# Gated linear attention and a mixture of experts: when the next group's x is split, and when the sums of H and L are added up

## The chip, the cores and the metric

The kernel runs on one core of one Trainium2 chip. The metric is the device time of one execution in microseconds, as the median of three runs. PE is TensorE, DVE is VectorE, ACT is ScalarE; PEld is PE's loading of weights.

## The reference

Two blocks follow one another. The first is a recurrence over 768 positions for each of 4 batches and 8 heads of 48 channels; the second is a sum of four two-layer networks (experts) on 3072 rows of 384, each weighted by a normalised probability:

```python
for t in range(S):
    state = alpha[:, :, t, :, None] * state + np.einsum('bhd,bhe->bhde', k[:, :, t], v[:, :, t])
    y[:, :, t] = np.einsum('bhd,bhde->bhe', q[:, :, t], state)
...
x = np.ascontiguousarray(attn_out.transpose(0, 2, 1, 3)).reshape(B * S, H * D)
...
p = domain_probs / (domain_probs.sum(-1, keepdims=True) + 1e-09)
for e in range(E):
    h = np.maximum(x @ w1[e], 0.0)
    out += p[:, e:e + 1] * (h @ w2[e])
```

Here w1[e] is 384 x 1024 and w2[e] is 1024 x 384. Everything is float32.

## The kernel before

**Tiling.** The 3072 rows are 24 blocks (units) of 128 rows. They are taken in seven groups of 2, 4, 4, 4, 4, 4 and 2 blocks, numbered 0 to 6. For each group the main loop (L704) runs over the four experts. For each expert it computes the first layer (`up`, eight tiles of 128 hidden channels, each for all rows of the group) and then the second (`down`, over the rows in turns of one or two blocks). The recurrence of the blocks of the next group (`attention`, a generator with 17 steps) is worked off meanwhile.

**Three parts of a number.** A product of 128x128 by 128x384 takes PE 0.33 us with float32 operands (ten start in 3.3 us at 157.0) and 0.18 us with operands of the type float32r[...]. So the kernel writes a number as three float32r parts: H (in the code `top`), the number times 1 − 1/8192 and rounded by the type; L (`low`), the number minus H; and D (`dif`), H/4096 − L. The product of two numbers is then got from three products of like parts: H by H and L by L go into one sum in PSUM, D by D into another, and the result is the first sum times 1 + 1/4096 plus the second. In `up` the two sums are `one` and `two`, in `down` they are `ops0` and `ops1`; the factor 1 + 1/4096 sits in `p_fine`, which is `p_all` times it. The first layer works in this way in groups 1 to 5 and in most of group 6, the second layer in groups 2 to 5. Elsewhere they use whole float32 numbers.

**The split of x.** `split_x` (L451) makes the three parts of the next group's x, one of three chunks of 128 channels at a time: `split` has ACT write H (L242), then DVE write L (L243) and D (L244). It is called during the last expert's `down` of a group, through a list `between` of fractions of the way through the turns at which the calls are made (L713 to L718). With three chunks these are 1/4, 2/4 and 3/4 of the whole `down`. The tile xT that it fills has one buffer, so it can't be filled before the last `up` of the group has read the old one.

**The second layer.** In groups 2 to 5 a turn of `down` takes two blocks (slots), so there are two turns, numbered 0 and 1. A turn has 48 products of 128x128 by 128x384, in the order of `steps` (L557): H and L for the first six hidden tiles of both slots, then H and L for the last two, then D for all eight of slot 0 and all eight of slot 1. Numbered from 0, the last product of slot 0's sum of H and L is step 29, of slot 1's 31; those of D are 39 and 47. The weights and the hidden tiles are there in three parts; D of the hidden tiles for slots 2 and 3 (`make_dif`, L538) is made during turn 0, one at every fifth step.

**The banks.** `one`, `two`, `ops0` and `ops1` share four PSUM banks (tag "g"), taken in rotation. A turn of `down` uses all four: slot 0's H-and-L sum, slot 0's D sum, slot 1's two. The next turn's first product therefore goes into the bank in which slot 0's H-and-L sum of this turn stands, and waits until that has been read. It is read by `add_up` (L592), which adds each sum, scaled by the row's probability, to `acc`: with a DVE operation (L603), or, for the first expert's first sum, with an ACT copy (L601). `add_up` stands after the last D product of a slot and takes both sums of that slot, one after the other.

**What sets the order.** The order on each engine is the order of the program text as it is run (a manual schedule). `advance` (L649), called before each product of `down` and after each tile of `up`, keeps a clock of estimated costs and runs the steps of `attention` that have come due by a list that `deal` (L619) makes. Attention's last step of a group is due 6 us (`MARGIN`) before the last expert's `down`. In groups 0 and 1, `background` also runs the splitting of the weights w1 and w2 into three parts (L218 to L224), which uses ACT and DVE.

**Names in the steps of the prediction.** qb and KT (L303, L321, L322) and QT and dec (L310, L312) are attention's copies and products per level; `near` (L339) takes the scores out of PSUM; `far` (L384), `sc` (L329) and `yps` (L416) are its products on PE. Within a step of attention, ACT copies QT to qb (L303) before DVE changes QT (L310). `hidden_parts` (L526) makes H, L and half of D of a hidden tile.

Of the kernel before, what the change touches and what calls it, by code (L numbers as in the profile page):

```python
# [14 lines left out]
ACT = mybir.ActivationFunctionType  # L15
ALU = mybir.AluOpType
# [4 lines left out]
def kernel(  # L21
# [37 lines left out]
    nc = tc.nc  # L59
# [9 lines left out]
    KC = DM // P  # L69
    FCH = F // P  # L70
# [9 lines left out]
    TRIM = 1 - 1 / 8192  # L80

    j = np.arange(P)[:, None] % HALF
    n = np.arange(QUAD)[None, :]
# [15 lines left out]
    p_all = const.tile([P, NBLK, E], F32, name="p_all")  # L99
    tot = const.tile([P, NBLK], F32, name="tot")  # L100
    p_fine = const.tile([P, NBLK, E], F32, name="p_fine")
# [27 lines left out]
    xTs = {}  # L129
    xraws = {}  # L130
# [105 lines left out]
            splitting.append(making.popleft())  # L236
            next(splitting[-1])

    def split(x, out):

        top, low, dif = out
        nc.scalar.activation(out=top, in_=x, func=ACT.Copy, scale=TRIM)  # L242
        nc.vector.tensor_sub(low, x, top.bitcast(F32))  # L243
        nc.vector.scalar_tensor_tensor(out=dif, in0=top.bitcast(F32), scalar=1 / 4096.0,  # L244
                                       in1=low.bitcast(F32), op0=ALU.mult, op1=ALU.subtract)
# [202 lines left out]
        load(u + 2, "v")  # L448
        yield

    def split_x(gi, which):  # L451
        n = len(groups[gi]) * P
        if 0 in which:
            xTs[gi] = work.tile([P, 3, KC, NT], F32R, name="xT", bufs=1)
        for kc in which:
            split(xraws[gi][:, kc, :n], [xTs[gi][:, part, kc, :n] for part in range(3)])


    def up(gi, e, fc, slots=None):
# [85 lines left out]
    def down(gi, e, slots, between):  # L545


        first = (gi * E + e) * NQ
        halves_ = split2(gi, e)
        if slots[0] == 0 and makes[1](gi, e):  # L550
            making.extend(split_piece(1, first + k) for k in range(NQ))
        if slots[0] == 0 and makes[0](gi, e) and 0 < e < E - 1:
            making.extend(split_piece(0, first + k) for k in range(2, NQ))
        sums = [[ps.tile([P, DM], F32, name=f"ops{j}", tag="g", bufs=4)
                 for j in range(2 if halves_ else 1)] for _ in slots]

        kinds = [((0, 1), range(FCH - 2)), ((0, 1), range(FCH - 2, FCH)), ((2,), range(FCH))]  # L557
        steps = [(part, i, fc) for parts, tiles in (kinds if halves_ else [((3,), range(FCH))])
                 for part in parts for i in range(len(slots)) for fc in tiles]
        for n, (part, i, fc) in enumerate(steps):  # L560
            c, f = divmod(fc, FPQ)
            h = hidden[c][:, :, f, slots[i] * P:(slots[i] + 1) * P]
            advance(cost(1, gi, e) / FCH / (3 if halves_ else 1))
            while between and n >= between[0][0] * len(steps):
                between.popleft()[1]()
            if n == len(steps) // 2:
                background()
            if later and n % 5 == 4:
                make_dif(*later.popleft())
            if halves_:  # L570
                w = wt[1][first + c].rearrange("p t (c d) -> p t c d", d=DM)[:, part, f]
                nc.tensor.matmul(sums[i][part // 2], lhsT=h[:, part], rhs=w,  # L572
                                 start=(fc == 0 and part != 1), stop=(fc == FCH - 1 and part != 0))
            else:
                w = wt[1][first + c].rearrange("p (c d) -> p c d", d=DM)[:, f]
                nc.tensor.matmul(sums[i][0], lhsT=h[:, 2].bitcast(F32), rhs=w,  # L576
                                 start=(fc == 0), stop=(fc == FCH - 1))
            if part >= 2 and fc == FCH - 1:
                add_up(gi, e, slots[i], sums[i])
        background()  # L580
        if slots[-1] == len(groups[gi]) - 1:
            while makes[1](gi, e) and (making or splitting):
                background()

            for c in range(NQ):
                del wt[1][first + c]
                if c < NQ // 2:
                    load_piece(1, first + NQ + c)
                else:
                    late.append(first + NQ + c)  # L590

    def add_up(gi, e, slot, sums):  # L592
        cb, b = groups[gi][slot]
        at = b * NCB + cb
        scales = (p_fine, p_all) if split2(gi, e) else (p_all,)
        if e == 0:
            accs[cb, b] = hid.tile([P, DM], F32, name="acc", bufs=B)
        acc = accs[cb, b]
        for j, (part, scale) in enumerate(zip(sums, scales)):
            if e == 0 and j == 0:  # L600
                nc.scalar.activation(out=acc, in_=part, func=ACT.Copy, scale=scale[:, at, e:e + 1])  # L601
            else:
                nc.vector.scalar_tensor_tensor(out=acc, in0=part, scalar=scale[:, at, e:e + 1],  # L603
                                               in1=acc, op0=ALU.mult, op1=ALU.add)
        if e == E - 1:
            del accs[cb, b]
            row = b * S + cb * P
            stores.append(lambda: (nc.sync if gi == len(groups) - 1 else nc.gpsimd).dma_start(
                out=out[row:row + P, :], in_=acc))
# [45 lines left out]
    with tc.manual_schedule():  # L655
        nc.scalar.dma_start(out=ident_all, in_=nc.inline_tensor(ident_np, name="ident_c").ap())
        nc.scalar.dma_start(out=masks, in_=nc.inline_tensor(mask_np, name="masks_c").ap())
        nc.scalar.dma_start(out=p_all, in_=moe_domain_probs.rearrange("(n p) e -> p n e", p=P))
        nc.gpsimd.memset(sts[B - 1], 0.0)
        for nm in "akq":  # L660
            for r in (early[nm], apart[nm]):
                nc.gpsimd.memset(r[:, :, D:], 0.0)
        nc.gpsimd.memset(lat[HALF:, :, :HALF], 0.0)
        for t in values + blocks:
            nc.gpsimd.memset(t, 0.0)
        for t in sts[:-1]:
            nc.gpsimd.memset(t, 0.0)

        load(0, "akqv")
        load(1, "akqv")  # L670
        for i in range(NQ):
            load_piece(0, i)

        idle = ps.tile([P, P], F32, name="idle", tag="g", bufs=4)
        zeros = sts[B - 1].rearrange("p a i d -> p (a i d)")[:, :P]

        def fill(n):
            for _ in range(n):  # L680
                nc.tensor.matmul(idle, lhsT=zeros, rhs=zeros, start=True, stop=True)

        runs = [attention(u) for u in range(len(groups[0]))]
        fill(8)
        for u, n in ((0, 3), (0, 6), (0, 4), (0, 5), (0, 5), (0, 4), (0, 3), (1, 0), (0, 0), (0, 2),
                     (0, 2), (1, 2), (0, 2), (1, 0), (0, 0), (0, 4), (0, 4), (0, 0)):
            next(runs[u])
            fill(n)
        norm_probs()

        span = cost(0, 0, 0) * FCH / 2 + cost(1, 0, 0)
        waiting.extend((span * (k + 1) / 15, u, runs[u])
                       for k, u in enumerate([1, 1, 1, 0, 1, 0, *[1] * 8]))
        for fc in range(FCH):
            up(0, 0, fc, slice(0, 1))
            advance(cost(0, 0, 0) / 2)
        down(0, 0, [0], deque())
        while waiting:
            next(waiting.popleft()[2], None)
        clock = 0.0  # L700
        waiting.extend((1.0 + k, 1, runs[1]) for k in range(2))
        waiting.extend(deal())

        for gi, e in ((gi, e) for gi in range(len(groups)) for e in range(E)):  # L704
            rest = gi == e == 0
            for fc in range(FCH):
                up(gi, e, fc, slice(1, len(groups[0])) if rest else None)
                advance(cost(0, gi, e) / (2 if rest else 1))
            each = 2 if split2(gi, e) else 1
            turns = [range(k, k + each) for k in range(rest, len(groups[gi]), each)]  # L710
            for k, slots in enumerate(turns):

                between = deque()  # L713
                if e == E - 1 and gi + 1 < len(groups):
                    for kc in range(KC):
                        at = (kc + 1) / (KC + 1) * len(turns) - k
                        if 0 <= at < 1:
                            between.append((at, lambda kc=kc: split_x(gi + 1, [kc])))  # L718
                down(gi, e, slots, between)
                if gi == len(groups) - 1 and e == E - 1:  # L720
                    stores.popleft()()
        while stores:
            stores.popleft()()
# [28 lines left out]
```

## Time and profile before

| | |
|---|---|
| median of 3 runs | 1102.42 us (1102.16 to 1103.28) |
| span of the profiled run | 1098.0 us |
| PE busy | 1066.2 us, 97% of the span |
| DVE busy | 751.9 us, 68% |
| ACT busy | 561.8 us, 51% |
| mean granted clock of PE | 0.995 |
| waits of PE for `add_up` | 11.9 us, 7 times |
| waits of PE for attention (`lat`, `qb`) | 12.4 us, all before 130 us |

A row of the costliest groups gives the line, the engine, the operation, output and inputs, the shapes and the count; then the busy time and the mean duration in ns; then the idle time of the engine just before these instructions, and whose end finished most of it. In the timeline the columns are start and length in us, the engine, the line, the operation, and in brackets the idle time before it with the one that ended it. Matmul ends are modelled, so idle time of PE is better read from starts. The granted clock is 1.00 at full speed.

### The profile page before, as it was taken

What the parts mean: (1) busy time and instruction counts of PE and PEld (TensorE: products, weight loads), DVE (VectorE), ACT (ScalarE), POOL (GpSimd) and SP (SyncE); (2) the same over time, 40 slices, a digit from 0 to 9 for tenths busy, and PEclk for the clock granted to TensorE, in tenths of its full rate; (3) what the DMA queues carried; (4) which work ended last, traced back from release to release, by engine and by line L of the source; (5) the groups of instructions that cost most, each with busy time, mean ns of one, the idle gap of its engine ahead of it and who ended that gap; (6) DMA issues with size and microseconds to landing.
All of it is one profiled execution on the core that took longest, in us unless ns stands there. A gap on an engine that the chain in (4) does not pass through costs nothing.

```text
span 1098.0 us, 21700 instructions
## 1 busy us (share of the span) xinstructions
PE 1066.2 (97%) x8532; PEld 894.9 (81%) x8532; DVE 751.9 (68%) x1625; ACT 561.8 (51%) x1191; POOL 35.4 (3%) x75
## 2 busy tenths in 40 slices
PE   8889899999999999998999999899999999999998
PEld 8767677676776889897898898798988898898876
DVE  5578777656558868768778777887786876657211
ACT  5786776575556554544545435455454354223321
POOL 2000000000000000000000000000000000000000
PEclk9999999999999999999999999999999999999999
DMA  8597689877696965855758649487487468555882
GB/s 124 156 322 231 206 283 370 307 269 275 206 314 213 405 234 186 335 206 207 287 170 308 246 147 352 143 277 302 146 292 290 176 270 343 221 200 243 300 317 87
DMA packets 166197, 273.68 MB, mean 249 GB/s; under 512 B 120624, under 2 KB 140976, under 8 KB 142032
## 3 DMA queue, kind: packets, MB, share of 16 engines
q1 hardware_dynamic: 156704, 230.06, 60.4%
q0 software_dynamic: 6016, 42.08, 9.6%
q8 instruction: 67, 1.10, 0.4%
q10 hardware_dynamic: 3376, 0.17, 0.3%
q14 instruction: 34, 0.28, 0.1%
HBM read 229.81 MB, written 42.47 MB: 248 GB/s over the span
## 4 chain that ended last, share of the span: by engine, by line
PE 77%; DVE 13%; ACT 6%; issue 2%; DMA 1%; SPq 0%; ACTq 0%; DVEq 0%
PE ops L572 19%; PE one L496 18%; PE ops L576 14%; PE two L496 9%; PE sc L329 5%; PE yps L416 4%; PE one L488 3%; DVE hT L530 3%; PE tp L261 3%; DVE t L505 2%; DVE hT L538 2%; ACT qb L303 2%; ACT hT L528 2%; DVE near L339 2%; PE sps L437 1%
## 5 line engine op out<-in xcount | busy, mean ns | idle before, releaser
L572 PE MATMUL ops<-w,hT 128*128 128x384 f32 x1536 | 288.6, 342 | 12.1 <-DVE acc L603 11.9
L572 PEld LDWEIGHTS ops<-w,hT 128*128 128x128 f32 x1536 | 268.1, 190 | 17.4 <-DVE acc L603 14.5
L496 PE MATMUL one<-xT,w 128*128 128x512 f32 (+1 forms) x1104 | 275.1, 385 | 0.1
L496 PEld LDWEIGHTS one<-xT,w 128*128 128x128 f32 x1104 | 194.8, 188 | 42.1 <-issue 3.0
L503 ACT ACTIVATE t<-one 128x512 f32<-128x512 f32 (+1 forms) x184 | 102.9, 559 | 158.5 <-PE one L496 158.0
L303 ACT COPY qb<-QT 64x256 f32<-64x256 f32 x336 | 136.5, 406 | 80.2 <-DVE QT L284 46.8
L576 PE MATMUL ops<-hT 128*128 128x384 f32 x512 | 176.2, 491 | 0.0
L496 PE MATMUL two<-xT,w 128*128 128x512 f32 (+1 forms) x552 | 148.5, 377 | 0.0
L576 PEld LDWEIGHTS ops<-hT 128*128 128x128 f32 x512 | 93.9, 191 | 56.1 <-issue 0.8
L530 DVE SCALAR_TENSOR_TENSOR hT<-t,hT 128x512 fp32r<-128x512 f32 x128 | 88.7, 693 | 61.3 <-ACT hT L528 59.9
L528 ACT ACTIVATE hT<-t 128x512 fp32r<-128x512 f32 x128 | 80.9, 632 | 96.9 <-DVE t L505 95.6
L496 PEld LDWEIGHTS two<-xT,w 128*128 128x128 f32 x552 | 100.3, 188 | 19.9
L603 DVE SCALAR_TENSOR_TENSOR acc<-ops,p_all,acc 128x384 f32<-128x384 f32 x88 | 54.2, 616 | 75.2 <-PE ops L576 43.6
L538 DVE SCALAR_TENSOR_TENSOR hT<-hT 128x256 fp32r<-128x256 f32 x256 | 100.9, 422 | 4.4
L505 DVE TENSOR_TENSOR t<-t,two 128x512 f32<-128x512 f32 x128 | 87.4, 682 | 20.9 <-PE two L496 12.7
L339 DVE COPY_PREDICATED near<-masks,sc 128x256 f32<-128x256 uint8 x144 | 77.0, 535 | 21.2 <-PE sc L329 18.2
L329 PEld LDWEIGHTS sc<-qb,KT 128*64 128x64 f32 x2304 | 73.0, 139 | 9.4 <-issue 7.4
L310 DVE TENSOR_TENSOR QT<-QT,dec 128x256 f32<-128x256 f32 x144 | 60.7, 422 | 24.8 <-ACT qb L303 24.2
L508 DVE TENSOR_TENSOR hT<-t,two 128x512 f32<-128x512 f32 (+1 forms) x56 | 32.1, 573 | 66.3 <-ACT t L503 56.5
L329 PE MATMUL sc<-qb,KT 128*64 128x64 f32 x2304 | 77.2, 224 | 0.3 <-ACT qb L303 0.3
L321 ACT COPY KT<-KT 128x256 f32<-128x256 f32 x144 | 59.8, 416 | 3.0
L322 DVE TENSOR_TENSOR KT<-KT,dec 128x256 f32<-128x256 f32 x144 | 60.2, 418 | 1.7 <-PE tp L261 1.5
(79 smaller groups left out, 928.1 us busy)
## 6 DMA issues: line engine op xcount, KB each, us to landing
w<-kept SPq DMA_DIRECT2D x156, 1152.0 KB
kept<-w POOLq DMA_DIRECT2D x32, 1152.0 KB, 7.5
hT<-in_moe_w_dram SPq DMA_DIRECT2D x48, 384.0 KB
w<-in_moe_w_dram SPq DMA_DIRECT2D x60, 128.0 KB
ra<-in_alpha_dram SPq DMA_DIRECT2D x23, 192.0 KB
rk<-in_k_dram SPq DMA_DIRECT2D x23, 192.0 KB
rq<-in_q_dram SPq DMA_DIRECT2D x23, 192.0 KB
out_dram<-acc POOLq DMA_DIRECT2D x22, 192.0 KB, 5.8
```

Of the source, the lines that this page charges most:

```text
L303: nc.scalar.copy(out=qb[rows, :, i, :].rearrange("p a (b r) -> p a b r", r=m), in_=qv[rows])
L310: nc.vector.tensor_mul(qv, qv, spread(dv[:, :, :, 0], m))
L329: nc.tensor.matmul(out[HALF * s:HALF * (s + 1), 2 * p:2 * p + 2, :], lhsT=KTs[li][:, p, HALF * s:HALF * (s + 1)], rhs=qbs[li][:, p, :, QUA ...
L339: nc.vector.copy_predicated(near.rearrange("p a (b two r) -> p a b two r", two=2, r=m)[:, :, :, 1, :], mk.unsqueeze(1).broadcast_to([P, H, ...
L496: nc.tensor.matmul(out, lhsT=w[:, part, kc], rhs=xTs[gi][:, part, kc, :n], start=(part == terms[0] and kc == 0), stop=(part == terms[-1] a ...
L503: nc.scalar.activation(out=t, in_=one, func=ACT.Copy, scale=FINE)
L505: nc.vector.tensor_add(t, t, two)
L528: nc.scalar.activation(out=top, in_=x, func=ACT.Relu, scale=TRIM)
L530: nc.vector.scalar_tensor_tensor(out=low, in0=x, scalar=0.0, in1=top.bitcast(F32), op0=ALU.max, op1=ALU.subtract)
L538: nc.vector.scalar_tensor_tensor(out=dif, in0=top.bitcast(F32), scalar=1 / 4096.0, in1=low.bitcast(F32), op0=ALU.mult, op1=ALU.subtract)
L572: nc.tensor.matmul(sums[i][part // 2], lhsT=h[:, part], rhs=w, start=(fc == 0 and part != 1), stop=(fc == FCH - 1 and part != 0))
L576: nc.tensor.matmul(sums[i][0], lhsT=h[:, 2].bitcast(F32), rhs=w, start=(fc == 0), stop=(fc == FCH - 1))
```

## The change

The three copies of H (one for each chunk) are no longer spread over the last `down`: all are made by ACT ahead of its first product (step 0 of `split_x`, at fraction 0). L and D of a chunk stay together on DVE (`split_rest`) and are made at 0.52, 0.62 and 0.72 of the way, which in two turns is in the first half of turn 1. What is left in `between` after a turn's last product is run there.

`add_up` now takes one sum. The sum of H and L (kind 0) is added once its last product has been issued, at step 29 for slot 0 and 31 for slot 1, and the sum of D (kind 1) at steps 39 and 47 as before. The aim is to have the banks of the H-and-L sums read sooner, and DVE's work on x out of the way of these additions. Where the second layer isn't in parts there is one sum, added as before.

```diff
-    def split(x, out):
+    def split_rest(x, out):
 
         top, low, dif = out
-        nc.scalar.activation(out=top, in_=x, func=ACT.Copy, scale=TRIM)
         nc.vector.tensor_sub(low, x, top.bitcast(F32))
         nc.vector.scalar_tensor_tensor(out=dif, in0=top.bitcast(F32), scalar=1 / 4096.0,
                                        in1=low.bitcast(F32), op0=ALU.mult, op1=ALU.subtract)
...
-    def split_x(gi, which):
+    def split_x(gi, step):
         n = len(groups[gi]) * P
-        if 0 in which:
+        if step == 0:
             xTs[gi] = work.tile([P, 3, KC, NT], F32R, name="xT", bufs=1)
-        for kc in which:
-            split(xraws[gi][:, kc, :n], [xTs[gi][:, part, kc, :n] for part in range(3)])
+            for kc in range(KC):
+                nc.scalar.activation(out=xTs[gi][:, 0, kc, :n], in_=xraws[gi][:, kc, :n],
+                                     func=ACT.Copy, scale=TRIM)
+        else:
+            kc = step - 1
+            split_rest(xraws[gi][:, kc, :n], [xTs[gi][:, part, kc, :n] for part in range(3)])
...
-            if part >= 2 and fc == FCH - 1:
-                add_up(gi, e, slots[i], sums[i])
+            if part >= 1 and fc == FCH - 1:
+                add_up(gi, e, slots[i], part // 2, sums[i][part // 2 if halves_ else 0])
+        while between:
+            between.popleft()[1]()
...
-    def add_up(gi, e, slot, sums):
+    def add_up(gi, e, slot, kind, part):
         cb, b = groups[gi][slot]
         at = b * NCB + cb
-        scales = (p_fine, p_all) if split2(gi, e) else (p_all,)
-        if e == 0:
+        if e == 0 and (kind == 0 or not split2(gi, e)):
             accs[cb, b] = hid.tile([P, DM], F32, name="acc", bufs=B)
         acc = accs[cb, b]
-        for j, (part, scale) in enumerate(zip(sums, scales)):
-            if e == 0 and j == 0:
-                nc.scalar.activation(out=acc, in_=part, func=ACT.Copy, scale=scale[:, at, e:e + 1])
-            else:
-                nc.vector.scalar_tensor_tensor(out=acc, in0=part, scalar=scale[:, at, e:e + 1],
-                                               in1=acc, op0=ALU.mult, op1=ALU.add)
+        scale = (p_fine if kind == 0 else p_all)[:, at, e:e + 1]
+        if e == 0 and (kind == 0 or not split2(gi, e)):
+            nc.scalar.activation(out=acc, in_=part, func=ACT.Copy, scale=scale)
+        else:
+            nc.vector.scalar_tensor_tensor(out=acc, in0=part, scalar=scale, in1=acc,
+                                           op0=ALU.mult, op1=ALU.add)
+        if kind == 0:
+            return
...
-                    for kc in range(KC):
-                        at = (kc + 1) / (KC + 1) * len(turns) - k
+                    for step, at in enumerate((0.0, 0.52, 0.62, 0.72)):
+                        at = at * len(turns) - k
                         if 0 <= at < 1:
-                            between.append((at, lambda kc=kc: split_x(gi + 1, [kc])))
+                            between.append((at, lambda step=step: split_x(gi + 1, step)))
                 down(gi, e, slots, between)
```

## The prediction

> **What bounds the kernel now.** First the page, for who is busy; then the waits of PE; then the program in order of time around the longest waits; last the granted clock there.
>
> ```profile
> PE 1066.2 (97%) x8532; PEld 894.9 (81%) x8532; DVE 751.9 (68%) x1625; ACT 561.8 (51%) x1191; POOL 35.4 (3%) x75
> L572 PE MATMUL ops<-w,hT 128*128 128x384 f32 x1536 | 288.6, 342 | 12.1 <-DVE acc L603 11.9
> ```
>
> PE is busy 97%; what an edit of DVE and ACT work can win lies in the other 3%. The second layer's row ends with PE's idle time before it: 12.1 us, all but 0.2 waiting for `add_up` on DVE. The waits of PE alone say how it is spread:
>
> ```profile
> PE ops L572 <- DVE acc L603: 11.9, 7, 3.8
> ```
>
> Seven waits. The timeline places them at 518.1 (3.76 us), 693.2 (3.76), 860.5 (1.91), 1008.9 (0.70), which are the last expert of groups 2 to 5, where the next x is split, and at 605.1 (0.71), 780.3 (0.71), 937.4 (0.40) in others. Each is before the second turn's first product: it needs the bank that held H and L of the first turn's slot 0. PE and DVE at the first one:
>
> ```profile
> 513.21 1.12 PE L572 MATMUL ops<-w,hT 128*128 128x384 f32 x5
> 518.09 4.79 PE L572 MATMUL ops<-w,hT 128*128 128x384 f32 x17 [3.76 <-DVE acc L603]
> ```
>
> ```profile
> 513.34 0.75 DVE L538 SCALAR_TENSOR_TENSOR hT<-hT 128x256 fp32r<-128x256 f32 x2
> 514.01 0.69 DVE L243 TENSOR_TENSOR xT<-x_raw,xT 128x512 fp32r<-128x512 f32 x1
> 514.73 0.69 DVE L244 SCALAR_TENSOR_TENSOR xT<-xT 128x512 fp32r<-128x512 f32 x1
> 515.34 0.75 DVE L538 SCALAR_TENSOR_TENSOR hT<-hT 128x256 fp32r<-128x256 f32 x2
> 516.01 0.42 DVE L310 TENSOR_TENSOR QT<-QT,dec 128x256 f32<-128x256 f32 x1
> 516.34 0.16 DVE L312 TENSOR_TENSOR dec<-dec 128x8 f32<-128x8 f32 x1
> 516.42 0.42 DVE L322 TENSOR_TENSOR KT<-KT,dec 128x256 f32<-128x256 f32 x1
> 516.75 0.75 DVE L538 SCALAR_TENSOR_TENSOR hT<-hT 128x256 fp32r<-128x256 f32 x2
> 517.42 0.61 DVE L603 SCALAR_TENSOR_TENSOR acc<-ops,p_fine,acc 128x384 f32<-128x384 f32 x1
> ```
>
> DVE has no gap: it is behind PE, and the addition that frees the bank stands last in a queue of other work, though its sum was complete 18 products earlier. PE stands from 514.33 to 518.09. What follows is the clock of PE in three stretches (start:end, us, PE busy, PEld busy, DVE, ACT, POOL, granted clock, DMA):
>
> ```profile
> 514.40:518.10 3.70, 0.01 (x1) 0.01 (x1) 3.60 (x10) 1.64 (x4) 0.00 (x0) 1.00 0.00 0
> 518.10:522.70 4.60, 4.60 (x17) 4.58 (x18) 4.38 (x9) 0.00 (x0) 1.08 (x2) 0.63 0.40 109
> 860.40:865.40 5.00, 4.88 (x79) 4.56 (x80) 4.71 (x11) 0.00 (x0) 1.08 (x2) 1.00 0.23 82
> ```
>
> After a 3.76 us wait 17 products take 4.6 us at a mean clock of 0.63; after the 1.91 us wait the clock stays 1.00. A product at full clock takes 0.178 us (48 in 8.88 us from 999.30, less the last one's 0.34), so 17 are worth 3.0 us: each long wait costs a further 1.6 us (at 693.2, 4.49 for 17: 1.5).
>
> [...]
>
> **The change part by part.**
>
> *Early addition of H and L.* No instruction is added; the two DVE additions per slot (0.61 and 0.62 us) stay, one moves 18 products (about 3.2 us) forward in program order. On DVE it now passes the last two L538 (0.67) and any attention step in between.
>
> *L and D later.* In groups 2 to 5 the first L243/L244 pair (0.72 + 0.61 = 1.33 us; half that for the short last group) leaves the first turn, behind its additions.
>
> *At 514.33:* of the DVE queue, 1.33 (L243, L244), 0.74 (L310 to L322) and 0.67 (last L538) now come after the addition: it starts at 517.42 − 2.74 = 514.68, ends 515.29, and PE goes on about 515.35. The wait is 1.0 us instead of 3.76 and the clock stays up: 2.74 + 1.6 = 4.3. The second slot's addition now follows at 515.21, and PE needs it six products later, 516.4.
>
> *What DVE takes back:* it has the same work in a shorter turn. Continuing its row from 515.2 with the durations above and the order of the built program, the H-and-L additions of turn two run 525.5 to 526.5, three attention steps (1.0) come next, and slot 0's D addition ends about 528.2. PE, without the slow clock, ends the turn at 515.35 + (530.32 − 518.09 − 1.6) = 526.0 and wants that D bank for the second sum of the next `up` at 527.4. I charge 0.8 us. Net 3.5 here, and 3.5 at 693, whose rows are the same within 0.05 us.
>
> *At 860.5:* the addition began at 859.86; less 1.33 and 0.67 it ends at 858.5, PE asks at 858.6: 1.9 saved. *1008.9:* short x, 1.4 us earlier: 0.7. *605.1, 780.3, 937.4:* the addition passes L538, and in the first two also L310 and L312, by 0.7 to 1.1 us: 0.71 + 0.71 + 0.40 = 1.8.
>
> *H at once.* Three ACT copies (L242, 0.63 us each, 0.53 apart: 1.6 us) stand ahead of attention's copies. In groups 2 to 5 ACT was idle in that place: at 509.50 it had waited 1.31 us for DVE, so qb starts 0.2 later. Group 1 has slack too (DVE idles 2.97 at 338.8). Group 0 has none:
>
> ```profile
> 159.15 0.81 ACT L303 COPY qb<-QT 64x256 f32<-64x256 f32 x2
> 160.30 0.63 ACT L242 ACTIVATE xT<-x_raw 128x512 fp32r<-128x512 f32 x1
> 160.56 0.42 DVE L310 TENSOR_TENSOR QT<-QT,dec 128x256 f32<-128x256 f32 x1
> 170.28 0.68 DVE L243 TENSOR_TENSOR xT<-x_raw,xT 128x512 fp32r<-128x512 f32 x1
> 170.57 1.65 PE L496 MATMUL one<-xT,w 128*128 128x512 f32 x6
> ```
>
> The copies go in ahead of the qb at 159.15, which then ends at 161.55; L310 overwrites what qb reads and starts 1.0 us late. Queued behind it on DVE is everything up to the last L at 170.28 (gapless till then), which group 1's first product already needs on arrival. PE loses 1.0 us. Bounds: 0, if a gap in DVE appears that I don't see, and 1.6, the whole of the copies.
>
> *A wait moved.* DVE may now stand at the H-and-L addition till PE gets there, with attention steps behind it. In turn one DVE is behind PE; in turn two it idles anyhow before the old place (1.48 us at 612.43). I charge nothing.
>
> Sum: 2 × 3.5 + 1.9 + 0.7 + 1.8 − 1.0 = 10.4 us; 1102.4 − 10.4 = 1092.0. With no bank wait and no loss in group 0 it is 13.0: 1089.4.
>
> **The rivals.**
> 1. *Both long waits and all short ones vanish wholly, group 0 costs nothing*: 1089. For: DVE had 0.55 and 1.43 us of gaps in turn two. Against: DVE's total work there hardly shrinks. 12%.
> 2. *DVE is the bound of the last second layer*: what is won at the second turn's start is given back at the next `up`, which waits for D's banks, and only the slow clock (3.1), half the short waits (2.2) and nothing else remain, less 1.0: 4.3 won, 1098. For: DVE runs gapless from 508 to 523. Against: its gaps. 15%.
> 3. *No change*: new waits of attention behind the early additions eat the rest; PE had no wait for attention after 130 us, but its slack isn't shown. 1102. 6%.
> 4. *Slower*: group 0 loses 1.6, and the H burst makes ACT the last to arrive at `far` or `yps` products in each of six groups, about 1.6 each[...]: 1106. For: before 130 us such waits exist (7.7 and 4.7 us in sum). Against: qb shifts by only 0.2 us. 7%.
>
> **How the numbers follow.** The forecast has 60%; its own spread (bank wait 0 to 1.6 per long event, group 0 loss 0 to 1.6) is 1089 to 1095. The range takes in rivals 1 and 2: 1087.5 to 1098.5. Faster by over 0.2% (2.2 us): 60 + 12 + 15 = 87%; within 6%; slower 7%.
>
> **What would show it.** In the trace after: the wait of L572's products for the addition falls from 11.9 to about 2 us; the clock stays 1.00 around 515 and 690; a new wait of `two` for the D addition, about 0.8 us, at the first product of groups 3 and 4; PE waits about 1.2 us for L at group 1's start instead of 0.2. Wrong would make me: [...]new waits of `sc`, `far` or `yps` after 130 us, or a DVE that stands at the early additions with L538 behind it.

## The result, and the profile after

The changed kernel takes 1087.04 us (median of 4 runs, 1086.73 to 1088.61); the kernel before, in the runs beside it, 1102.29 (1099.53 to 1103.28). The ratio is 0.9868, with a 95% interval of 0.9848 to 0.9889: 15.3 us by the medians, 12 to 17 by the interval. In the two profiled runs the span fell from 1098.0 to 1085.3, by 12.7. The forecast was 10.4 us, 1092.0. The measured time as it stands lies 0.5 us below the low end of the forecast's range; taken as a ratio to the 1102.42 from which the forecast started, it is 1087.9 and just inside.

First the page and the waits of PE, by the rows that answer to those shown of before:

```profile
PE 1062.9 (98%) x8532; PEld 892.9 (82%) x8532; DVE 747.7 (69%) x1625; ACT 560.7 (52%) x1191; POOL 35.3 (3%) x75
L576 PE MATMUL ops<-w,hT 128*128 128x384 f32 x1536 | 284.7, 340 | 2.1 <-DVE acc L609 2.1
```

```profile
PE ops L576 <- DVE acc L609: 2.1, 2, 1.1
```

The counts of instructions are the same to the last one. The idle time of PE before the second layer's products fell from 12.1 us to 2.1, and seven waits became two, of 1.11 and 1.01 us. PE in order of time at the first long place (columns: start, length, engine, line, operation; in brackets the idle time before it):

```profile
514.19 1.12 PE L576 MATMUL ops<-w,hT 128*128 128x384 f32 x5
516.42 3.21 PE L576 MATMUL ops<-w,hT 128*128 128x384 f32 x17 [1.11 <-DVE acc L609]
...
523.44 3.81 PE L576 MATMUL ops<-w,hT 128*128 128x384 f32 x20
527.11 1.65 PE L500 MATMUL one<-xT,w 128*128 128x512 f32 x6
528.60 0.85 PE L500 MATMUL two<-xT,w 128*128 128x512 f32 x3
529.45 1.67 PE L500 MATMUL one<-xT,w 128*128 128x512 f32 x6
```

VectorE beside it:

```profile
513.28 0.41 DVE L321 TENSOR_TENSOR KT<-KT,dec 128x256 f32<-128x256 f32 x1
513.62 0.90 DVE L338 COPY_PREDICATED near<-masks,sc 128x256 f32<-128x256 uint8 x2
514.42 1.42 DVE L542 SCALAR_TENSOR_TENSOR hT<-hT 128x256 fp32r<-128x256 f32 x4
515.76 1.13 DVE L609 SCALAR_TENSOR_TENSOR acc<-ops,p_fine,acc 128x384 f32<-128x384 f32 x2
516.81 0.41 DVE L309 TENSOR_TENSOR QT<-QT,dec 128x256 f32<-128x256 f32 x1
...
526.45 1.13 DVE L609 SCALAR_TENSOR_TENSOR acc<-ops,p_fine,acc 128x384 f32<-128x384 f32 x2
527.50 0.41 DVE L309 TENSOR_TENSOR QT<-QT,AT 128x256 f32<-128x256 f32 x1
527.84 0.42 DVE L311 TENSOR_TENSOR dec<-AT 128x256 f32<-128x256 f32 x1
528.17 0.42 DVE L321 TENSOR_TENSOR KT<-KT,AT 128x256 f32<-128x256 f32 x1
528.51 1.13 DVE L609 SCALAR_TENSOR_TENSOR acc<-ops,p_all,acc 128x384 f32<-128x384 f32 x2
```

The addition that frees the bank is now behind four steps of `make_dif` (L542), with no work on x in the queue; two steps of attention (L321, L338) are still ahead of it. The granted clock of the 17 products that follow the wait (start:end, us, busy time of PE, PEld, DVE, ACT and POOL, clock, DMA share, GB/s):

```profile
516.40:519.40 3.00, 2.98 (x17) 2.98 (x18) 2.97 (x9) 0.81 (x2) 0.27 (x1) 1.00 0.00 0
```

Seventeen products take 3.0 us again, where they took 4.6 at 0.63. In group 0, the three copies of H stand where they were foreseen to stand (first three lines ACT and DVE, the last PE):

```profile
159.22 1.66 ACT L456 ACTIVATE xT<-x_raw 128x512 fp32r<-128x512 f32 x3
160.78 0.81 ACT L302 COPY qb<-QT 64x256 f32<-64x256 f32 x2
161.62 0.43 DVE L309 TENSOR_TENSOR QT<-QT,dec 128x256 f32<-128x256 f32 x1 [0.91 <-ACT qb L302]
...
172.08 1.21 PE L500 MATMUL one<-xT,w 128*128 128x512 f32 x4 [0.80 <-DVE xT L242]
```

Where the 12.7 us came from is read by setting the starts of the phases (`up` and `down` of each group and expert) of the two profiles side by side:

| place | what changed there | us |
|---|---|---|
| group 0, H at once (0.90 from 157 us on) | lost | −0.97 |
| 518, the long wait | 4.19 won, 0.43 given back in the next `up` | 3.76 |
| 693, the long wait | 4.14 won, 0.25 given back in the next `up` | 3.89 |
| 860 | won | 2.02 |
| 1009 | won | 1.01 |
| 605, 637, 780, 937, the short waits | 0.95, 0.39, 0.96, 0.64 won | 2.94 |
| sum | | 12.65 |

Each of the two profiled runs had lost the clock once in the start-up (0.50 for 3.41 us, from 81.94 before and from 123.60 after), so that this hardly enters the table: at 157.0 us they stand 0.07 us apart.

### The profile page after: what moved, and what is told of

The parts are those of the page before. It is cut to its first block, busy times and chain, and to the rows that moved or that the text cites. A ratio compares the mean times of both kernels' runs of the same rounds, so it can differ in the third digit from the quotient of the medians.

```text
span 1085.3 us, 21700 instructions
## 1 busy us (share of the span) xinstructions
PE 1062.9 (98%) x8532; PEld 892.9 (82%) x8532; DVE 747.7 (69%) x1625; ACT 560.7 (52%) x1191; POOL 35.3 (3%) x75
## 4 chain that ended last, share of the span: by engine, by line
PE 87%; ACT 5%; DVE 5%; issue 2%; POOL 0%; ACTq 0%; DVEq 0%; POOLq 0%
PE ops L576 24%; PE one L500 21%; PE ops L580 13%; PE two L500 10%; PE sc L328 6%; PE yps L415 4%; PE one L492 3%; PE tp L260 3%; ACT qb L302 2%; PE sps L436 1%; PE far L383 1%; PE idle L689 1%; DVE near L338 1%; DVE hT L534 1%; DVE t L509 1%
## 5 line engine op out<-in xcount | busy, mean ns | idle before, releaser
L576 PE MATMUL ops<-w,hT 128*128 128x384 f32 x1536 | 284.7, 340 | 2.1 <-DVE acc L609 2.1
L532 ACT ACTIVATE hT<-t 128x512 fp32r<-128x512 f32 x128 | 80.9, 632 | 95.8 <-DVE t L509 94.6
L542 DVE SCALAR_TENSOR_TENSOR hT<-hT 128x256 fp32r<-128x256 f32 x256 | 101.3, 421 | 4.4
L338 DVE COPY_PREDICATED near<-masks,sc 128x256 f32<-128x256 uint8 x144 | 77.0, 535 | 17.6 <-PE sc L328 14.5
L309 DVE TENSOR_TENSOR QT<-QT,dec 128x256 f32<-128x256 f32 x144 | 60.7, 421 | 32.5 <-ACT qb L302 32.0
L321 DVE TENSOR_TENSOR KT<-KT,dec 128x256 f32<-128x256 f32 x144 | 60.1, 417 | 2.2 <-PE tp L260 2.2
```

The costliest lines, as they stand in the source:

```text
L309: nc.vector.tensor_mul(qv, qv, spread(dv[:, :, :, 0], m))
L338: nc.vector.copy_predicated(near.rearrange("p a (b two r) -> p a b two r", two=2, r=m)[:, :, :, 1, :], mk.unsqueeze(1).broadcast_to([P, H, ...
L532: nc.scalar.activation(out=top, in_=x, func=ACT.Relu, scale=TRIM)
```

## The experiments

The theory: the addition that frees the next turn's bank waits behind the work that stands ahead of it in VectorE's order; the change takes work from ahead of it, and where a wait had let the clock drop, that cost goes too. The rivals: VectorE is the bound there, so that what is won comes back as another wait; or one half of the change does all the work.

### Each half alone

The first kernel has the early addition and leaves the split of x as it was, H, L and D of a chunk together (H is copied at the head of `split_rest` again, which is not shown):

```diff
...
-                    for step, at in enumerate((0.0, 0.52, 0.62, 0.72)):
+                    for step, at in enumerate((0.25, 0.5, 0.75)):
```

> Only the early addition of the H and L sums; x is split as before the change, in thirds. Theory (queue on DVE plus clock): at the two long places the pair L, D of the first third (1.33 us) is ahead of the addition again, so PE idles about 3.76 - 1.41 = 2.35 us there, which keeps the clock up: 2.9 won at each; 0.7 at group 4, 1.0 at group 5, 2.9 at the three short places; no loss of 1.0 at the start of group 1. Sum about 10 us against the kernel before, 1092. Rival (the early addition is the whole change, the split is beside the point): all 12.7 of the profiled gain and the 1.0 of group 1 on top, 1088. Rival (the clock drops also after 2.35 us): 3 us less, 1095.

Measured: 1092.24 us (1089.6 to 1095.04), ratio 0.9903 (0.9886 to 0.992), span 1090.2. Its waits of PE for the addition:

```profile
PE ops L572 <- DVE acc L605: 5.8, 3, 2.3
```

The second has the moved split, and adds both sums after D as before:

```diff
-            if part >= 1 and fc == FCH - 1:
-                add_up(gi, e, slots[i], part // 2, sums[i][part // 2 if halves_ else 0])
+            if part >= 2 and fc == FCH - 1:
+                for kind in ((0, 1) if halves_ else (1,)):
+                    add_up(gi, e, slots[i], kind, sums[i][kind if halves_ else 0])
```

> Only the moved split of x; both sums are added after the D products as before the change. Theory: the addition still stands behind all eight L538, but no longer behind the first L, D pair: PE idles about 3.76 - 1.33 = 2.43 us at the long places, with the clock up: 2.9 won at each, 1.3 at group 4, 0.8 at group 5, nothing at the three short places, 1.0 lost at the start of group 1. Sum about 7 us, 1095. The two parts alone then add up to about 17, more than the 12.7 of both, because each by itself is enough to keep the clock up. Rival (shares simply add): 12.7 minus what the other part alone gives, about 2.7. Rival (the clock drops after 2.43 us): 4 us, 1098.

Measured: 1096.22 us (1094.64 to 1098.87), ratio 0.9943 (0.9929 to 0.9957), span 1094.5. PE at its waits:

```profile
519.26 3.22 PE L576 MATMUL ops<-w,hT 128*128 128x384 f32 x17 [2.45 <-DVE acc L610]
604.93 2.04 PE L576 MATMUL ops<-w,hT 128*128 128x384 f32 x10 [0.71 <-DVE acc L610]
691.50 4.80 PE L576 MATMUL ops<-w,hT 128*128 128x384 f32 x17 [2.43 <-DVE acc L610]
```

The first came out as expected, 1092 us with the clock up at both long places (waits of 2.34 us; at the second of them 17 products in 3.24); the second is 1.2 us above the 1095 that was expected, and lost the clock at one of its two. That waits of 2.35 and 2.43 us keep the clock up was the author's estimate, between the 1.91 and the 3.76 us of the kernel before; it held at three of these four waits. That either half is the whole change is refuted. At the long places the queue adds up: 3.76 us before, less 1.42 (to 2.34, the early addition alone), less 1.31 (to 2.45, the moved split alone), would leave 1.03; both together leave 1.11 and 1.01. The short waits in the other experts (0.71 at 604.93) go with the early addition alone; this kernel still has them. The times of the halves don't simply add: by the medians 10.5 and 6.5 us alone (against 1102.7 of the kernel before beside them) and 15.3 both, by the starts of the phases from 157 us on, past the start-up, 9.8 and 5.4 alone and 12.8 both. The halves together give more than the whole, as was expected, because keeping the clock up at a long place can be won only once. (The whole spans, 7.8 and 3.5 against 12.7, say the opposite, but both halves lost the clock twice in the start-up and the other two kernels once; the mean clocks of the halves, 0.996 and 0.995, fit that together with the stretch after 691.50.) In the kernel with the moved split a wait of 2.43 us at 691.50 was followed by 4.80 us for 17 products, one of 2.45 at 519.26 by 3.22. What decides whether the clock drops is told in the last section.

### Group 0 spread out

The changed kernel, but with the x of group 1 split in thirds as before:

```diff
-            for kc in range(KC):
+            for kc in range(KC if gi > 1 else 0):
...
+            if gi == 1:
+                nc.scalar.activation(out=xTs[gi][:, 0, kc, :n], in_=xraws[gi][:, kc, :n],
+                                     func=ACT.Copy, scale=TRIM)
...
-                    for step, at in enumerate((0.0, 0.52, 0.62, 0.72)):
+                    for step, at in enumerate((0.0, 0.52, 0.62, 0.72) if gi else (0.24, 0.25, 0.5, 0.75)):
```

> The changed kernel, but the x of group 1 is split in thirds as before the change, H with its L and D; the other groups are as changed. Theory: the burst of three H copies on ACT is what delays group 1's start, so the 0.97 us come back and PE's wait for L at the first product of group 1 falls from 0.8 to about nothing: 1.0 us faster than the changed kernel, 1086. Rival (it is not the burst on ACT but L and D being later on DVE): the delay comes back as well, since L and D move with it; told apart in the trace by when ACT frees QT: QT's product on DVE at about 160.6 without a gap in front of it if it was the burst.

Measured: 1086.82 us (1086.41 to 1091.39), ratio 0.9866 (0.9846 to 0.9885), span 1087.5. Not measurably faster. From 157 us to group 1's first `down` it lost 0.6 us against the kernel before, where the changed kernel lost 0.9. The product of QT on VectorE (L309, at 163.28 in this trace) starts without a gap again, which tells the burst of copies on ACT from the later L and D. The wait for L went, and PE met another one soon after,

```profile
178.81 1.62 PE L503 MATMUL one<-xT,w 128*128 128x512 f32 x6 [0.68 <-DMA w<-kept]
```

This is a weight that comes by DMA. So the loss in group 0 has the cause that the prediction named, but undoing the cause wins only 0.3 us of it.

### The D of the hidden tiles later

Four steps of `make_dif` stand ahead of the early addition (1.42 us at 514.42). They are needed only in turn 1's last products, so this kernel begins with them after the additions:

```diff
-            if later and n % 5 == 4:
+            if later and n % 5 == 4 and (slots[0] > 0 or n > 31):
```

> The changed kernel, but D of the hidden tiles for slots 2 and 3 (L538 of the kernel before) is made from step 34 of turn 0 on instead of from step 4, so at most none of it stands ahead of the early additions. Theory A (only the order of DVE's queue matters): the two waits left at the long places (1.1 and 1.0 us of idle, 2.8 on the weight loads) vanish and the kernel gains 2.5 us: 1084.5. Theory B (in the last second layer of groups 2 and 3 DVE is full, so the same work only comes later): the waits at turn 1 vanish but PE waits at the next first layer's first product instead, for the same addition of turn 1 or for L and D of x; gain 0 to 0.7: 1086.5 to 1087. B is the likelier, as DVE has no gap from 509.7 to 529.6 in the changed kernel.

Measured: 1088.19 us (1086.93 to 1088.78), ratio 0.9868 (0.9853 to 0.9882), span 1086.3. The waits for the addition are gone, and PE waits as long for the D instead:

```profile
526.61 1.83 PE L576 MATMUL ops<-w,hT 128*128 128x384 f32 x9 [1.19 <-DVE hT L542]
```

So the remaining 1.1 us comes from the amount of VectorE's work in this `down`, and this change of its order only moved the wait.

### More work in VectorE's queue

The opposite test: five subtractions of 128x256 that nothing needs, ahead of the early addition in the last expert's turn 0.

```diff
+            if part == 1 and fc == FCH - 1 and i == 0 and e == E - 1 and slots[0] == 0:
+                for _ in range(5):
+                    nc.vector.tensor_sub(xTs[gi + 1][:, 1, 0, :256], xraws[gi + 1][:, 0, :256],
+                                         xTs[gi + 1][:, 0, 0, :256].bitcast(F32))
             if part >= 1 and fc == FCH - 1:
```

> The changed kernel, with five more VectorE subtractions of 128x256 (about 0.34 us each, 1.7 us) queued ahead of the early addition of slot 0's H and L in each last second layer of a group; they write into the next group's x before its L and D do, so nothing of the output changes. Theory (at these places the time goes with VectorE's queue, us for us, once it is full): the two waits of 1.1 us grow to about 2.8, each place loses 1.7 us, the other places (605, 780, 860, 937, 1009), whose queue is emptier, lose 0.5 to 0.8 us each, so 1087.0 and 5 to 6 make 1092 to 1093, and 1.6 us more for each place at which the clock drops. Rival (TensorE's products wait for something else, and VectorE has slack): under 1 us more.

Measured: 1099.36 us (1096.18 to 1102.21), ratio 0.9971 (0.9962 to 0.9979), span 1097.7: most of the gain is gone, 12.4 us by the spans. PE and, in the first line, VectorE:

```profile
517.09 2.25 DVE L584 TENSOR_TENSOR xT<-x_raw,xT 128x256 fp32r<-128x256 f32 x5
519.93 4.74 PE L576 MATMUL ops<-w,hT 128*128 128x384 f32 x17 [3.28 <-DVE acc L613]
693.26 3.21 PE L576 MATMUL ops<-w,hT 128*128 128x384 f32 x17 [3.18 <-DVE acc L613]
858.72 2.94 PE L576 MATMUL ops<-w,hT 128*128 128x384 f32 x9 [1.95 <-DVE acc L613]
1008.46 8.65 PE L576 MATMUL ops<-w,hT 128*128 128x384 f32 x48 [1.46 <-DVE acc L613]
```

The dose was 2.25 us, not 1.7, and the long waits grew by 2.17 each: the queue goes into PE's wait us for us. The expectation's 5 to 6 us was too small in three ways: the dose; the slack at 860 and 1009, which was only 0.3 and 0.8 us (waits of 1.95 and 1.46 us came up); and the clock, which dropped after the wait of 3.28 us and after that of 1.95, but not after that of 3.18. It also counted 605, 780 and 937, which this edit doesn't touch, since it acts in the last expert alone. Extra waits 7.75 (9.87 in all, less 2.12), two cold stretches at 1.5 and 1.1 (4.74 less 3.21; 2.94 less 1.83), and 1.3 that the profiled run had already lost when group 1 began make 11.7 of the 12.4; the nine products end 0.9 us before the half clock does, so the second stretch is sized too small.

### L and D of x on GpSimd

If VectorE's load is what remains, another engine could take it; `pool` holds for the groups from the fourth on:

```diff
+        if pool:
+            nc.gpsimd.tensor_sub(low, x, top.bitcast(F32))
+            nc.gpsimd.tensor_scalar_mul(out=dif, in0=top.bitcast(F32), scalar1=1 / 4096.0)
+            nc.gpsimd.tensor_sub(dif, dif.bitcast(F32), low.bitcast(F32))
+            return
...
-                    for step, at in enumerate((0.0, 0.52, 0.62, 0.72)):
+                    for step, at in enumerate((0.0, 0.02, 0.03, 0.04) if gi > 1 else (0.0, 0.52, 0.62, 0.72)):
```

> The changed kernel, with L and D of x of the groups from the fourth on made by GpSimd (three operations for each tile of 128x512, instead of VectorE's two), right behind H, so that VectorE has no work on x at the two long places. Theory (VectorE's queue is what is left there: it ran without a gap from 509.7 to 529.6, and the two waits of 1.1 us and the give-back of 0.43 and 0.25 us in the next 'up' both come from it): both waits go below 0.3 us and the give-back goes, 2 to 3 us, about 1084.5 where the changed kernel has 1087.0. Rival 1 (the wait is that of the last products for the chain hidden tile, D of it, addition, whatever else VectorE has): the waits stay at 1.0 to 1.1 and the time within 0.5 us. Rival 2 (GpSimd is so slow at these, or slows VectorE beside it by so much, that L and D are not there at the next group's start): a new wait of the next group's first products for xT, and 1088 or more.

Measured: 1109.03 us (1108.25 to 1110.39), ratio 1.0059 (1.0042 to 1.0076): slower than the kernel before. None of the three had it; the second rival came nearest, for VectorE was slowed, but the next group found its xT in time, and it was the waits for the addition that grew. The rows of this kernel, of GpSimd (POOL), VectorE and PE in order of time:

```profile
510.95 1.42 POOL L243 TENSOR_TENSOR xT<-x_raw,xT 128x512 fp32r<-128x512 f32 x1 [147.59 <-ACT xT L461]
511.14 1.51 DVE L314 TENSOR_TENSOR QT<-QT,dec 128x256 f32<-128x256 f32 x1
...
516.88 1.55 POOL L244 TENSOR_SCALAR xT<-xT 128x512 fp32r<-128x512 f32 x1
517.84 0.41 DVE L326 TENSOR_TENSOR KT<-KT,dec 128x256 f32<-128x256 f32 x1
518.96 3.58 DVE L548 SCALAR_TENSOR_TENSOR hT<-hT 128x256 fp32r<-128x256 f32 x4
519.73 1.45 POOL L243 TENSOR_TENSOR xT<-x_raw,xT 128x512 fp32r<-128x512 f32 x1
...
523.12 5.23 PE L582 MATMUL ops<-w,hT 128*128 128x384 f32 x17 [6.75 <-DVE acc L615]
```

A VectorE operation that takes 0.42 us elsewhere began 0.19 us after GpSimd's subtraction, took 1.51 us, and ended 0.28 us after it; four of `make_dif` took 3.58 us, which took 1.42 in the changed kernel. Over that whole kernel one of `make_dif` takes 0.475 us on average, in the changed kernel 0.421. So VectorE's operations took longer beside GpSimd's subtractions; by what mechanism the trace doesn't show. Beside its scaling by a constant (L244, one input) not all of them did: a VectorE product of two inputs (L326) ran inside it and kept its 0.41 us. So the work left VectorE's queue and its time stayed there, longer than before: GpSimd's three operations take about 4.3 us for what VectorE did in 1.3, and most of VectorE's work beside them is drawn out. Waits of 6.75, 6.54, 3.42 and 1.19 us (15.8 more than in the changed kernel) and cold clocks after the first three of them (5.7) make 21.5 us; by the starts of the phases it lost 21.2 us from 505 us on, and 1.1 before. That fits a wait set by VectorE's queue. That relieving the queue would bring 2 to 3 us was not tried in a form that relieves it, nor was GpSimd tried with this work in turn 1, where the changed kernel has it; here it stands in turn 0, ahead of the early addition.

### The clock in the start-up

Times of one kernel differ by up to 6 us between runs. In the profiled runs the differences by 142 us already reach 2.7 us: PE waits 2.74 and 3.50 us for copies of `lat` at 80.9 and 123.2, and in some runs the clock is one half for 3.41 us after one, or the other, or both: in the kernel before from 81.94, in the changed one from 123.60, in its second profiled run from 80.9 and from 125.3. With group 0 spread out it was longer once: 60 products took 5.66 us from 124.84, the same ones 3.06 from 124.73 in the kernel before. To test it, these waits are filled with products that nothing uses and that the real ones overwrite:

```diff
         yps = ps.tile([P, KC, P], F32, name="yps", tag="w")
+        for _ in range({2: 20, 4: 26}.get(u, 0)):
+            nc.tensor.matmul(yps[:, 0, :], lhsT=ident, rhs=ident, start=True, stop=True)
```

> The changed kernel, with 20 and 26 products of 128x128 that nothing uses laid into the two waits of TensorE for ScalarE's copies of lat during the start-up (2.74 us at 80.9 and 3.50 us at 123.2; at 0.11 us for each they fill 2.2 and 2.9 us of them, and the real products overwrite them). Theory (a granted clock of one half for about 4 us after one or the other of these waits, in some executions and not in others, is what spreads the times of a kernel): the clock stays at 1.00 from 80 to 130 us, 1.6 us for each cold stretch, so about 1085.0 where the changed kernel has 1087.0, and the runs of it lie within 1 us of each other. Rival (the spread has another source, and these waits cost only their own length): the same time within 0.5 us, the same spread of 2 to 5 us.

Measured: 1088.81 us, and all runs between 1088.59 and 1088.95; ratio 0.9874 (0.9857 to 0.9892). The spread is gone and the clock is 1.000 over the whole run, but the median isn't lower: each of these products took 0.23 us in two passes, and 20 and 26 of them outlasted the waits by 1.50 and 1.87 us. Together with the GpSimd split:

> Both together: L and D of x on GpSimd from the fourth group on, and the two waits of the start-up filled with products that nothing uses. Where both theories hold, the gains add up, for they lie at different times: 1087.0 less 2.5 less 2.0, about 1082.5. Where only one does, 1084.5 to 1085; where neither, 1087.

Measured: 1110.08 us (1108.6 to 1111.88), ratio 1.0066 (1.005 to 1.0083): the same as the GpSimd split alone. Neither theory brought a gain here: the filling in this dose costs about what it saves, as it did alone. Then half the dose, beside the unaltered changed kernel on the same chip:

```diff
-        for _ in range({2: 20, 4: 26}.get(u, 0)):
+        for _ in range({2: 10, 4: 13}.get(u, 0)):
```

> The changed kernel once more, unaltered, to stand beside the next one on the same chip. Its record so far: 1087.04 (1086.73 to 1088.61) and ratio 0.9868. If the clock in the start-up is the source of the spread, its times lie between 1085.5 and 1090, in steps of about 1.6 us for each of the two waits after which the clock drops; the rival, another source, has no such steps.

> The changed kernel with 10 and 13 products of 128x128 that nothing uses in the two waits of the start-up. With 20 and 26 each took 0.23 us (two passes), twice what was reckoned, so that they outlasted the waits by 1.50 and 1.87 us; the clock stayed at 1.00, the times lay within 0.4 us, and the median was 1088.8. Half of them take 2.3 and 3.0 us and end before the waits do (2.74 and 3.50 us). Theory: the clock stays at 1.00 still, and 1088.8 less 3.4 gives 1085.4, with a spread under 1 us; against the changed kernel beside it 1.5 to 2.5 us less. Rival (the remaining idle time of 0.4 to 0.5 us, or the half-filled waits, lets the clock drop all the same): 1087 with the same spread as the changed kernel.

The changed kernel: 1087.81 us (1086.57 to 1090.02), ratio 0.9871 (0.9851 to 0.9891). With half the filling: 1085.23 us (1084.73 to 1085.63), ratio 0.9845 (0.9828 to 0.9863), the fastest of all. PE's clock after the two waits, first in the changed kernel, then with the filling (start:end, us, PE busy, clock, DMA share, GB/s):

```profile
81.00:85.00 4.00, 4.00 (x46) 0.58 0.32 108
125.00:129.00 4.00, 4.00 (x59) 0.57 0.85 330
```

```profile
80.00:85.00 5.00, 4.48 (x105) 1.00 0.36 116
122.00:129.00 7.00, 6.38 (x131) 1.00 0.62 242
```

In this profiled run of the changed kernel the clock fell after both waits; the spans are 1086.6 and 1083.5, 3.1 us apart, twice 1.6. For the changed kernel the clock in the start-up is shown to be the main source of the spread: with it held up, the spread falls from 3.5 us to 0.9. The steps of 1.6 us that the expectation spoke of can't be told in its four times (1086.57, 1087.29, 1088.34, 1090.02), but the mean granted clocks of these four runs fall as the times rise: 0.998, 0.998, 0.997 and 0.995.

## Why the prediction was right, and where it was small

**The long waits.** Right, and nearly to the number. Counting back from the queue, it had the early addition start 0.35 us after PE stands, a wait of 1.0 us and the clock up; measured were 1.11 and 1.01, the clock 1.00, and 4.19 and 4.14 us won at each place, against 2.74 + 1.6 = 4.3.

**The charge for D's bank, 0.8 us each.** The effect exists, its size was wrong, and so was its place. The prediction let the first `two` of the next group begin at 527.4 and wait for the bank until 528.2 by its own reckoning. In the trace after, `two` begins at 528.60, before slot 0's D addition, the first of the pair at 528.51 (about 0.6 us long), can be done: it doesn't need that bank. A strict rotation of the four banks, as the text ahead of the prediction has it, would have given `two` just this bank; so the banks are handed out in another order here, which the trace doesn't show. The trace has no new wait of `two`. The next `up` gives back 0.43 and 0.25 us, most of it at the second `one` (529.45), which starts 0.05 us after ACT has read out the first (528.80 for 0.60 us). ACT did not read late: it had been idle, and began as soon as the first `one` was complete. Why the second `one` waits for it isn't shown. With the early addition alone there is no give-back (0.01 us in that trace). This term was 0.9 us too dear in the sum.

**860.5 and 1008.9.** 1.9 and 0.7 forecast, 2.02 and 1.01 measured.

**The short waits.** This is the term that was most mis-sized: 1.8 us forecast, 2.94 measured. The forecast took the idle times of the row of matmuls, 0.71 + 0.71 + 0.40, although their ends are modelled. The row of weight loads of the kernel before shows them longer, and one more:

```profile
PEld ops L572 <- DVE acc L603: 14.5, 8, 4.1
```

Eight waits and 14.5 us, against seven and 11.9. The extra one, of 0.4 us, is at 646.8, in the second layer that begins at 637.7; at 605.1 the weight loads waited 0.96 us where the matmuls show 0.71. The time won, 0.95, 0.39, 0.96 and 0.64, follows that row.

**Group 0.** Right: 1.0 us forecast, 0.90 measured from 157 us on; L309 was put 1.0 us later and started at 161.62. The forecast wait for L at group 1's start of 1.2 us shows as 0.80 by the matmuls and 1.2 by the weight loads. What it didn't see is that a weight's DMA can stand right behind it, as in the kernel with group 0 spread out.

**A wait moved: nothing charged.** Right: no new waits of `sc`, `far` or `yps` after 130 us, and VectorE's additions wait no longer for the sums of the products in parts than before (30.2 us after, 30.9 before).

**The rivals.** The second, that VectorE gives all back in the next `up`, is refuted in its size: 0.68 us came back of 8.3. Its premise, VectorE full, is right: later D of the hidden tiles only moved the wait, and 2.25 us more work came out as 2.17 us more wait. The first had the time within 2 us, by the wrong sum: it took the waits to vanish, and 2.1 us of them are left. Neither the third nor the fourth shows anywhere.

**From 12.7 to 15.3 us.** The sum of the trace is 12.7; the medians say 15.3, 14.5 in the second comparison (1102.29 and 1087.81). The profiled run of before, 1099.81 us, lies at the low end of that kernel's times (1099.32 to 1105.74 over all the runs of it), that of the changed kernel, 1087.1, near its median. The longer runs have no trace, but each of the runs beside the experiments has its mean granted clock, and the times go with it: runs of the kernel before at 0.995 took 1099.3 to 1100.5 us, at 0.994 1100.8 to 1103.0, at 0.992 1101.8 to 1104.1, and at 0.989 1105.2 to 1105.7. A half-clock stretch of 3.41 us makes 0.0016 of a run's mean clock. So the forecast started from a median, 1102.4, that holds by this estimate one or two such stretches more than the profiled run whose waits it summed. In which places they lie, and how many of them the change removes, isn't shown.

## What to carry to other kernels

Where an engine that takes its work in the order of the program, as VectorE's rows show it here, releases a buffer, count what is queued ahead of the releasing instruction from the moment when its data was complete: the wait followed the sum of their durations to within about 0.1 us here, with work taken away and with work added. Where matmul ends are modelled, look at the waits of the weight loads as well, and compare the starts of whole phases, which also show what is given back. Before shifting the load to another engine, look whether its work slows the first: here a chunk's 1.3 us of VectorE work became about 4.3 us on GpSimd, and a VectorE operation of 0.42 us beside it took 1.51.

## What the runs showed of the hardware

**The clock and where a wait falls.** The prediction took a wait of 3.76 us to drop the clock and one of 1.91 not to, as the kernel before shows both; where between them the limit lies, no run had shown. The length alone doesn't decide there: the clock dropped after 1.95, 2.43, 2.73, 3.28 and 3.50 us and stayed up after 1.91, 2.34, 2.45, 2.74, 3.18 and 3.49. But the traces show what does. Half clock comes in stretches of 3.41 us (or twice that: 6.84 from 520.7 in the kernel with GpSimd), and within a run their starts lie whole multiples of 3.413 us apart: in the kernel before at 81.94, 518.85 and 692.93, which are 128 and 51 of them. Laid over the whole run, this grid of windows cuts a wait into parts. The first two rows are two of these stretches in the kernel before (start:end, us, PE busy, PEld, DVE, ACT, POOL, clock, DMA share, GB/s). The next two are the wait of 1.95 us in the kernel with more in VectorE's queue and what follows it; the last three are the wait of 3.49 us before 124.73 in the kernel before and what follows that:

```profile
518.85:522.26 3.41, 3.41 (x13) 3.41 (x12) 3.24 (x6) 0.00 (x0) 1.08 (x2) 0.50 0.46 115
692.93:696.34 3.41, 3.11 (x10) 3.11 (x11) 3.16 (x7) 0.14 (x1) 0.54 (x1) 0.50 0.29 80
855.71:859.12 3.41, 1.46 (x9) 1.14 (x8) 3.27 (x9) 0.99 (x2) 0.00 (x0) 1.00 0.00 0
859.12:862.53 3.41, 3.41 (x27) 2.97 (x27) 3.38 (x9) 0.00 (x0) 1.07 (x2) 0.50 0.16 59
119.49:122.90 3.41, 1.75 (x14) 0.85 (x12) 2.34 (x7) 3.33 (x9) 0.00 (x0) 1.00 0.69 260
122.90:126.31 3.41, 1.58 (x56) 1.47 (x56) 2.56 (x7) 2.95 (x7) 0.53 (x1) 1.00 0.56 223
124.70:128.70 4.00, 3.97 (x66) 2.92 (x66) 2.30 (x7) 2.67 (x7) 0.18 (x1) 1.00 0.86 332
```

The wait of 1.95 us lies whole in one window (3.41 less the busy 1.46), and the next window has half clock. The wait of 3.49 us is cut into 1.66 and 1.83, and the clock stays at 1.00, also from 124.7 on, where the changed kernel's, after the same wait, was shown above at 0.57. In eight traces (before, after, the second of the changed kernel, more in VectorE's queue, both with GpSimd, both with filling alone), from 60 to 1080 us, 18 windows at full clock hold 1.95 us or more of PE's idle time, and each is followed by half clock. No other window at full clock is; the longest idle times in those are 1.83, 1.79, 1.67 and 1.66 us. So in these runs a wait dropped the clock when 1.95 us or more of it, 57% of a window, fell into one window, and 1.83 us or less did not. An estimate from these figures, with 1.9 us for the limit: under it a wait is safe, over twice that it always costs the clock, and between them it is a matter of where the grid lies, which differs from run to run; it is then best counted as its length plus a share of 1.6 us.

**Products that nothing uses.** A float32 product of 128x128 by 128x128 took 0.23 us, two passes of 0.115: in the kernel with half the filling thirteen are 26 matmuls, 2.99 us from the first start at 119.05 to the next product's at 122.04. Ten and thirteen of them, 5.4 us of useless work in all, saved 2.6 us by the medians.
